# A fused attention and gated FFN kernel: loads in one ordered queue far ahead, first two batches turned in 64x64 quarters, FFN groups spread evenly

## The chip, the cores and the metric

The kernel runs on one core of one Trainium2 chip. The metric is device time in microseconds (us) from the first to the last instruction of one execution. Five engines work side by side, each through its own instructions in strict order: TensorE (PE in the profile; its weight loads are PEld), VectorE (DVE), ScalarE (ACT), GpSimd (POOL) and SyncE (SP). SyncE computes nothing here; it issues all DMA transfers. An instruction waits until the buffers it reads are filled and the buffers it writes are free, and everything behind it on its engine waits with it.

## The reference: what is computed

Eight batches of eight heads with 576 tokens and head size 64 go through causal attention with 16 extra "beacon" keys that every query may see. The result, put together over the heads (4608 tokens by 512), goes through an FFN with a ReLU gate.

```python
k_all = concat([beacon_k, k]); v_all = concat([beacon_v, v])      # per batch and head
scores = q @ k_all.T / 8, later keys masked out (never the beacons)
a = softmax(scores);  attn = a @ v_all                            # (8, 8, 576, 64)
x = attn as (4608, 512)
out = (relu(x @ w_gate) * (x @ w_val)) @ w_out                    # 512 -> 1536 -> 512, float32
```

Inputs and output are float32; matmuls run in bf16 and accumulate in float32.

## The kernel before

Everything is emitted in one hand-made order (`manual_schedule`), so the Python order is the order on each engine. Names used below:

- A **burst** is one pair of heads and one of two groups of query rows of a batch: 8 bursts a batch, 64 in all. `qk` makes the scores on TensorE, `softmax` does exp on ScalarE and masks the causal edge on GpSimd (`affine_select`), `av` multiplies with V a burst later and VectorE scales the result into `x`.
- A **tick** is one turn of the main loop: one burst, some FFN groups beside it, and loads for later batches. Bursts 0 to 7 (batch 0) come ahead of the loop, ticks 8 to 15 hold batch 1, five ticks have no burst, then batches 2 to 7 follow.
- An FFN **token tile** is 512 tokens; nine of them. Each has 12 gate/value groups (`up`, 8 matmuls of 128x128 by 512) and 4 `down` groups (12 such matmuls).

Loads come as float32 into a staging buffer `stg` and are cast to bf16. For batches 0 and 1, keys and queries are loaded a pair of heads at a time and turned by TensorE; for later batches they are loaded as row tiles ("pieces"), cast by GpSimd and turned by a DMA transpose. The attention result `x` is turned into `xT` by DMA transposes, all issued by SyncE.

```python
stage = main.enter_context(tc.tile_pool(name="stage", bufs=9))     # tiles of 128 x 768 float32
...
def pair_kq(b, p, src):                       # 96 partitions, runs of 1536 bytes
    t = stg()
    nc.sync.dma_start(t[:96].rearrange("p (h x) -> p h x", h=2),
                      src[b, 2 * p:2 * p + 2].rearrange("h (p r) d -> p h (r d)", r=R))   # R = 6
    return t

def turn_kq(t, dst, eng, cp):
    c = c16t()
    eng.tensor_copy(c[:96].rearrange("p (r h d) -> p r h d", r=R, h=2), t[:96]...)
    tp = f_ps.tile([P, R, 96], BF16, name="f")
    for r in range(R):                        # 6 transposes of 96 x 128
        nc.tensor.transpose(tp[:, r], c[:96, r * P:(r + 1) * P], ident[:96, :96])
    cp(dst.rearrange("q (p r) -> q p r", r=R), tp.rearrange("q r p -> q p r"))
# ... (cut)
def softmax(u, i):
    segs, cols = SLABS[u.g][i]                # two slabs a burst, two score buffers s_ps
    p = psb.tile([P, 2, 512], BF16, name="p")
    A.activation(p[:, :, :cols], u.s[i][:, :, :cols], AF.Exp, scale=scale)
    for (kt, q0, n, c, mask) in segs:
        if mask:
            G.affine_select(out=p[:, :, c:c + m], ...)
# ... av(u): matmuls, then VectorE; after the last pair of a group:
        if u.last:
            for qi in qt:
                r0, rn = QROWS[qi]
                nc.sync.dma_start_transpose(xT[:, :, u.b * S + r0:u.b * S + r0 + rn], u.x[:rn, qi, :])
# ... FFN
def up(nf):
    g = f_ps.tile(...)                        # 4 matmuls with wg
    A.activation(gs, g, AF.Relu)
    u = f_ps.tile(...)                        # 4 matmuls with wv
    V.tensor_mul(st["h"][:, nf, :], gs, u)
def down(ms):
    o = f_ps.tile(...)                        # 12 matmuls with wo
    A.copy(ob, o)
    nc.sync.dma_start(out[...], ob)
return [(1.74, up(nf)) for nf in range(NF)] + [(2.6, down(ms)) for ms in range(4)]   # (cost in us, emit)
```

The schedule of batches 0 and 1, and of the main loop:

```python
turn_beacons(bk, 0); pair_turn(0, 0, *loads[0])        # k cast by V, q by G
load_v_half(0, 0)                                      # V of four heads, cast by G
for s in range(8):
    u = bursts[s]; start(u); qk(u); softmax(u, 0)
    if s == 0: nxt(0, 1); load_v_half(0, 4)            # nxt: load a pair and turn it
    if s in (2, 4): nxt(0, s // 2 + 1)
    softmax(u, 1)
    if s: av(bursts[s - 1], o_ps if s % 2 else f_ps)
av(bursts[7], o_ps)                                    # then the DMA transposes of batch 0
for c, w in wq:
    if c < 2: w()(V)                                   # load gate and value weights, cast by V
# five FFN groups of tile 0, then beacons, pairs, V of batch 1 and the other weights ... (cut)
for s, u in enumerate(ticks, 8):
    if u: start(u); qk(u); softmax(u, 0)
    if prev:
        av(prev, o_ps)
        if prev.last: ...                              # a token tile becomes ready two ticks later
            ffn += [(s + 2, *g) for g in ffn_tile(m)]
    prev = u
    budget = 1.7 if s < 16 else 4.0
    spent = 0.0
    while spent < budget and ffn and ffn[0][0] <= s:   # FFN groups while there are any
        _, cost, g = ffn.pop(0); g(); spent += cost
        ...                                            # softmax(u, 1) after 1.7 us of them
    # pairs 2, 3 and V of batch 1 at s = 8, 10; three wo loads a tick from s = 10 ... (cut)
    for x in turned: piece_turn(x)                     # DMA transposes of pieces cast a tick ago
    while inflight and inflight[0][0] <= s:            # cast pieces loaded a tick or two ago (G)
        ...
    if s >= 14:                                        # load 3 pieces a tick early on, later 2
        ...
while ffn:
    if len(ffn) == 6: in_range = count_in_range()      # VectorE, TensorE, VectorE, then a register load
    ffn.pop(0)[2]()
```

The range check at the end counts rows whose sums of exp are in a sane range; a general path follows for inputs where they aren't, and isn't taken here.

Of the kernel before, what the change touches and what calls it, by code (L numbers as in the profile page):

```python
# [10 lines left out]
FP32 = mybir.dt.float32  # L11
# [131 lines left out]
def kernel(  # L143
# [15 lines left out]
    P = 128  # L159
# [9 lines left out]
    R = S // 96  # L169
# [27 lines left out]
    stage = main.enter_context(tc.tile_pool(name="stage", bufs=9))  # L197
# [9 lines left out]
    def stg():  # L207
        return stage.tile([P, 768], FP32, name="stg")

    def c16t():  # L210
        return c16.tile([P, 768], BF16, name="c16")

    V, G, A = nc.vector, nc.gpsimd, nc.scalar


    def pair_kq(b, p, src):
        t = stg()
        nc.sync.dma_start(t[:96].rearrange("p (h x) -> p h x", h=2),
                          src[b, 2 * p:2 * p + 2].rearrange("h (p r) d -> p h (r d)", r=R))
        return t  # L220

    def turn_kq(t, dst, eng, cp):
        c = c16t()
        eng.tensor_copy(c[:96].rearrange("p (r h d) -> p r h d", r=R, h=2),  # L224
                        t[:96].rearrange("p (h r d) -> p r h d", r=R, h=2))
        tp = f_ps.tile([P, R, 96], BF16, name="f")
        for r in range(R):
            nc.tensor.transpose(tp[:, r], c[:96, r * P:(r + 1) * P], ident[:96, :96])  # L228
        cp(dst.rearrange("q (p r) -> q p r", r=R), tp.rearrange("q r p -> q p r"))

    def rows_of(src, b, h0, h1, s0, s1):
        return src[b, h0:h1, s0:s1].rearrange("h p d -> p h d")

    def tile_rows(t, src, beacon, b, h0, h1, st):
        dst = st[:, :H * D].rearrange("p (h d) -> p h d", d=D)[:, h0:h1]
        if beacon is None:
            s0, n = t * P, min(P, S - t * P)
            nc.sync.dma_start(dst[:n], rows_of(src, b, h0, h1, s0, s0 + n))
            return n
        if t == 0:  # L240
            nc.sync.dma_start(dst[:Nb], rows_of(beacon, b, h0, h1, 0, Nb))
            nc.sync.dma_start(dst[Nb:], rows_of(src, b, h0, h1, 0, P - Nb))
            return P
        s0 = t * P - Nb
        n = min(P, S - s0)
        nc.sync.dma_start(dst[:n], rows_of(src, b, h0, h1, s0, s0 + n))  # L246
        return n

    def cast_v(eng, st, b, t, n, h0=0, h1=H):
        eng.tensor_copy(vs[b % 2][:n, t, h0:h1, 0:D],  # L250
                        st[:n, :H * D].rearrange("p (h d) -> p h d", d=D)[:, h0:h1])

    def load_w(dst, src, ko0, nko, n0, nn):
        t = stg()
        w = t[:, :nko * nn].rearrange("p (k n) -> p k n", k=nko)
        nc.sync.dma_start(w, src.rearrange("(ko ki) n -> ki ko n", ki=P)[:, ko0:ko0 + nko, n0:n0 + nn])
        return lambda eng: eng.tensor_copy(dst[:, ko0:ko0 + nko, n0:n0 + nn], w)  # L257
# [28 lines left out]
    def av(u, opool):  # L286
# [29 lines left out]
        if u.last:  # L316
            for qi in qt:
                r0, rn = QROWS[qi]
                nc.sync.dma_start_transpose(xT[:, :, u.b * S + r0:u.b * S + r0 + rn], u.x[:rn, qi, :])  # L319
# [38 lines left out]
    def count_in_range():  # L358

        cols = B * NP * NKT * 2  # L360
        flat = rall.rearrange("p b n t a -> p (b n t a)")
        ge = const.tile([P, cols], FP32, name="ge")
        V.tensor_scalar(out=ge, in0=flat, scalar1=1e-10, scalar2=None, op0=ALU.is_ge)
        V.scalar_tensor_tensor(out=ge, in0=flat, scalar=1e10, in1=ge, op0=ALU.is_le, op1=ALU.mult)
        ok = const.tile([P, 1], BF16, name="ok")
        V.tensor_reduce(ok, ge, op=ALU.min, axis=AX.X)
        cnt_ps = o_ps.tile([1, 1], FP32, name="o")
        nc.tensor.matmul(cnt_ps, ok, ones, start=True, stop=True)
        cnt = const.tile([1, 1], mybir.dt.int32, name="cnt")
        V.tensor_copy(cnt, cnt_ps)  # L370
        return nc.values_load(cnt, min_val=0, max_val=P,
                              skip_runtime_bounds_check_because="a count of rows")

    with tc.manual_schedule():


        def beacons_k(b):
            t = stg()
            nc.sync.dma_start(t[:Nb, :H * D].rearrange("p (h d) -> p h d", d=D), rows_of(beacon_k, b, 0, H, 0, Nb))
            return t  # L380

        def turn_beacons(t, b):
            c = c16t()
            V.tensor_copy(c[:Nb, :H * D], t[:Nb, :H * D])
            tp = f_ps.tile([P, NP, Nb], BF16, name="f")
            for p in range(NP):
                nc.tensor.transpose(tp[:, p], c[:Nb, p * P:(p + 1) * P], ident[:Nb, :Nb])
            V.tensor_copy(kTs[b % 2][:, :, 0:Nb], tp)

        def pair_turn(b, p, tk, tq):  # L390
            turn_kq(tk, kTs[b % 2][:, p, Nb:Stot], V, V.tensor_copy)
            turn_kq(tq, qTs[b % 2][:, p, :], G, V.tensor_copy)

        bursts = []
        xs = {}
# [13 lines left out]
        ffn = []  # L409

        bk = beacons_k(0)
        loads = [(pair_kq(0, 0, k), pair_kq(0, 0, q))]
        vst = {}
        def load_v_half(b, h0):
            for t in range(NKT):
                if t not in vst:
                    vst[t] = stg()
                n = tile_rows(t, v, beacon_v, b, h0, h0 + 4, vst[t])
                cast_v(G, vst[t], b, t, n, h0, h0 + 4)
            if h0:  # L420
                vst.clear()

        turn_beacons(bk, 0)
        pair_turn(0, 0, *loads[0])
        prev = None

        def nxt(b, p):
            tk, tq = pair_kq(b, p, k), pair_kq(b, p, q)
            pair_turn(b, p, tk, tq)

        wq = []
        for c in range(4):
            n0 = c * (d_ff // 4)
            for ko in (0, 2):
                for dst, src in ((wg, moe_w_gate), (wv, moe_w_val)):
                    wq.append((c, lambda dst=dst, src=src, ko=ko, n0=n0: load_w(dst, src, ko, 2, n0, d_ff // 4)))

        load_v_half(0, 0)
        for s in range(8):
            u = bursts[s]  # L440
            start(u)
            qk(u)
            softmax(u, 0)
            if s == 0:
                nxt(0, 1)
                load_v_half(0, 4)
            if s in (2, 4):
                nxt(0, s // 2 + 1)
            softmax(u, 1)
            if s:  # L450
                av(bursts[s - 1], o_ps if s % 2 else f_ps)
        av(bursts[7], o_ps)
        for c, w in wq:
            if c < 2:
                w()(V)
        ffn += [(0 if j < NF else 16, *g) for j, g in enumerate(ffn_tile(0))]
        for _ in range(5):
            ffn.pop(0)[2]()
        vst.clear()
        bk = beacons_k(1)  # L460
        turn_beacons(bk, 1)
        nxt(1, 0)
        load_v_half(1, 0)
        for c, w in wq:
            if c == 2:
                w()(V)
        nxt(1, 1)
        for c, w in wq:
            if c == 3:
                w()(V)  # L470
        wo_loads = [lambda f=f: load_w(wo, moe_w_out, f, 1, 0, d_model) for f in range(NF)]

        pieces = []
        for b in range(2, B):
            for t in range(NKT):
                for nm in "kqv":
                    pieces.append((b, t, nm))
        inflight, turned = [], []

        def piece_load(x):  # L480
            b, t, nm = x
            st = stg()
            src, be = {"k": (k, beacon_k), "q": (q, None), "v": (v, beacon_v)}[nm]
            n = tile_rows(t, src, be, b, 0, H, st)
            return (b, t, nm, n, st)

        def piece_cast(x):
            b, t, nm, n, st = x
            if nm == "v":
                cast_v(G, st, b, t, n)  # L490
                return None
            c = c16t()
            G.tensor_copy(c[:n, :d_model], st[:n, :d_model])  # L493
            return (b, t, nm, n, c)

        def piece_turn(x):
            b, t, nm, n, c = x
            dst = (kTs if nm == "k" else qTs)[b % 2]
            nc.sync.dma_start_transpose(dst[:, :, t * P:t * P + n], c[:n, :d_model])  # L499

        GAP = 5
        ticks = bursts[8:16] + [None] * GAP + bursts[16:] + [None]
        begin = {b: 8 + GAP + 8 * (b - 1) for b in range(2, B)}
        done_at = {}
        prev = None
        for s, u in enumerate(ticks, 8):
# [4 lines left out]
            if prev:  # L511
                av(prev, o_ps)
                if prev.last:
# [9 lines left out]
            while spent < budget and ffn and ffn[0][0] <= s:  # L523
# [3 lines left out]
                if sm and spent >= 1.7:  # L527
                    softmax(u, 1)
                    sm = False
# [59 lines left out]
```

## Time and profile before

| | |
|---|---|
| time, median of 2 runs | 476.27 us (475.24 to 477.31) |
| span of the profiled run | 476.1 us, 7626 instructions |
| TensorE busy | 390.8 us (82%), mean granted clock 0.896 |
| ScalarE, VectorE, GpSimd busy | 188.7, 156.9, 127.9 us |
| DMA moved | 60.17 MB, mean 126 GB/s |

The page cuts the span into 40 slices and gives the busy share of each engine in tenths; PEclk is the clock that the throttle granted to TensorE, DMA the mean share of the 16 DMA engines. A list of waits gives, for every engine, whom it waited for: total us, count, longest. An order in time has one line per group of instructions: start us, us, engine, line of the kernel, operation, out<-in, count, and in brackets the idle time before it and what ended it. SPq lines are DMA issues on SyncE. Windows give for one stretch the busy time and count of PE, PEld, DVE, ACT and POOL, then the clock, the DMA share and GB/s.

### The profile page before, as it was taken

How to read it: one execution, taken by the hardware profiler on the slowest of the kernel's cores; microseconds unless marked ns; L12 is line 12 of the kernel's file. 1: busy time of each engine (PE TensorE's matmuls, PEld its weight loads, DVE VectorE, ACT ScalarE, POOL GpSimd, SP SyncE). 2: the span in 40 equal slices, each digit the busy share in tenths (PEclk: the TensorE clock that was granted, in tenths of full speed). 3: DMA queues.
4: the chain of work that ended last, by engine and by line, in shares of the span. 5: the costliest groups of instructions: out<-in, count | busy, mean ns of one | idle time of the engine just before them, and what ended most of it. 6: DMA issues, size and time to landing. Idle time of an engine off the chain costs nothing.

```text
span 476.1 us, 7626 instructions
## 1 busy us (share of the span) xinstructions
PE 390.8 (82%) x2830; PEld 194.7 (41%) x2873; DVE 156.9 (33%) x362; ACT 188.7 (40%) x273; POOL 127.9 (27%) x288
## 2 busy tenths in 40 slices
PE   2760917889986855999999999689979998999975
PEld 1450313444432433445444544434443445544432
DVE  3441455570330121341342342224222422430430
ACT  2440202471350642454553554535453545532311
POOL 4530203233134434331432333422342212000000
PEclk9975765899997955899999999979997998999999
DMA  9507989646998789943893753966495004002002
GB/s 188 116 10 179 262 219 228 227 93 127 221 176 168 184 122 165 169 78 92 178 193 94 170 117 92 183 134 117 102 197 109 18 29 94 2 19 89 1 1 92
DMA packets 160554, 60.17 MB, mean 126 GB/s; under 512 B 147200, under 2 KB 154368, under 8 KB 160512
## 3 DMA queue, kind: packets, MB, share of 16 engines
q1 hardware_dynamic: 160512, 59.63, 60.0%
q8 instruction: 24, 0.39, 0.4%
q14 instruction: 18, 0.15, 0.1%
HBM read 38.27 MB, written 9.44 MB: 100 GB/s over the span
## 4 chain that ended last, share of the span: by engine, by line
PE 65%; DMA 14%; SPq 9%; DVE 3%; issue 3%; ACT 3%; POOL 2%; DVEq 0%; POOLq 0%; ACTq 0%
PE f L332 18%; PE f L338 18%; PE f L347 17%; PE o L304 6%; PE s L270 5%; SPq L319 4%; DMA stg<-in_v_dram 4%; DMA stg<-in_k_dram 3%; DMA xT<-x 3%; ACT p L277 2%; DMA stg<-in_q_dram 2%; SPq L246 1%; DMA stg<-in_moe_w_out_dram 1%; DMA stg<-in_moe_w_gate_dram 1%; SPq L499 1%
## 5 line engine op out<-in xcount | busy, mean ns | idle before, releaser
L332 PE MATMUL f<-xT,wg 128*128 128x512 bf16 x406 | 117.0, 404 | 23.1 <-DVE wg L257 12.5
L277 ACT ACTIVATE p<-s 128x992 bf16<-128x992 f32 (+2 forms) x128 | 107.4, 864 | 65.6 <-PE s L270 65.3
L340 DVE TENSOR_TENSOR hT<-g,f 128x512 bf16<-128x512 f32 x108 | 74.2, 688 | 147.8 <-PE f L338 133.4
L335 ACT ACTIVATE g<-f 128x512 f32<-128x512 f32 x108 | 64.5, 597 | 136.3 <-PE f L332 128.9
L338 PE MATMUL f<-xT,wv 128*128 128x512 bf16 x427 | 116.1, 394 | 1.5 <-ACT ob L350 0.8
L281 POOL TENSOR_SCALAR_AFFINE_SELECT p<-p 128x256 bf16<-128x256 bf16 (+2 forms) x160 | 61.4, 398 | 189.9 <-ACT p L277 186.2
L347 PE MATMUL f<-wo,hT 128*128 128x512 bf16 x420 | 97.1, 385 | 0.8 <-issue 0.2
L332 PEld LDWEIGHTS <-wg 128*128 128x128 bf16 x432 | 41.9, 103 | 70.4 <-DVE wg L257 13.1
L338 PEld LDWEIGHTS <-wv 128*128 128x128 bf16 x432 | 44.1, 102 | 58.3 <-issue 11.8
L304 PE MATMUL o<-vx,p 128*128 128x65 bf16 (+2 forms) x906 | 48.2, 208 | 19.0 <-POOL p L281 15.5
L347 PEld LDWEIGHTS <-hT 128*128 128x128 bf16 x432 | 42.0, 99 | 49.6 <-issue 3.0
L304 PEld LDWEIGHTS <-p 128*128 128x128 bf16 (+2 forms) x960 | 42.3, 115 | 33.5 <-POOL p L281 18.3
L312 DVE RECIPROCAL rall<-o 128x2 f32<-128x2 f32 (+2 forms) x90 | 15.7, 174 | 115.2 <-PE o L304 113.9
L350 ACT COPY ob<-f 128x512 f32<-128x512 f32 x36 | 21.1, 586 | 80.5 <-PE f L347 54.4
L270 PE MATMUL s<-qT,kT 64*128 64x208 bf16 (+4 forms) x512 | 42.0, 280 | 6.7 <-ACT p L277 5.2
L493 POOL CAST c<-stg 128x512 bf16<-128x512 f32 (+2 forms) x60 | 36.1, 613 | 40.2 <-DMA stg<-in_k_dram 28.5
L313 DVE TENSOR_TENSOR x<-o,rall 128x128 bf16<-128x128 f32 (+2 forms) x90 | 34.6, 384 | 3.3
L270 PEld LDWEIGHTS <-kT 64*128 64x128 bf16 x512 | 21.0, 102 | 30.1 <-issue 25.8
L250 POOL CAST vx<-stg 128x512 bf16<-128x512 f32 (+3 forms) x50 | 26.2, 529 | 13.9 <-DMA stg<-in_v_dram 13.7
L228 PE MATMUL f<-ident,c 96*128 96x96 bf16 x96 | 8.9, 252 | 23.0 <-DVE c L224 16.8
L224 POOL CAST c<-stg 96x768 bf16<-96x768 f32 x8 | 6.6, 822 | 40.5 <-DMA stg<-in_q_dram 40.4
L228 PEld LDWEIGHTS <-c 96*128 96x128 bf16 x96 | 6.1, 119 | 26.8 <-DVE c L224 19.5
(30 smaller groups left out, 44.8 us busy)
## 6 DMA issues: line engine op xcount, KB each, us to landing
out_dram<-ob SPq DMA_DIRECT2D x36, 256.0 KB, 2.3
stg<-in_q_dram SPq DMA_DIRECT2D x24, 256.0 KB, 4.0
stg<-in_k_dram SPq DMA_DIRECT2D x18, 256.0 KB, 3.9
stg<-in_v_dram SPq DMA_DIRECT2D x18, 256.0 KB, 4.1
stg<-in_moe_w_gate_dram SPq DMA_DIRECT2D x8, 384.0 KB, 4.6
stg<-in_moe_w_val_dram SPq DMA_DIRECT2D x8, 384.0 KB, 5.1
stg<-in_moe_w_out_dram SPq DMA_DIRECT2D x12, 256.0 KB, 5.8
stg<-in_k_dram SPq DMA_DIRECT2D x8, 288.0 KB, 4.9
```

The lines of the kernel that those rows point to most:

```text
L250: eng.tensor_copy(vs[b % 2][:n, t, h0:h1, 0:D], st[:n, :H * D].rearrange("p (h d) -> p h d", d=D)[:, h0:h1])
L270: nc.tensor.matmul(s[:, a, c:c + n], kTs[u.b % 2][rows, u.pi, kt * P:(kt + 1) * P], qTs[u.b % 2][rows, u.pi, q0:q0 + n], start=True, stop= ...
L277: A.activation(p[:, :, :cols], u.s[i][:, :, :cols], AF.Exp, scale=scale)
L281: G.affine_select(out=p[:, :, c:c + m], in_=p[:, :, c:c + m], pattern=[[0, 2], [1, m]], compare_op=ALU.is_ge, fill=0.0, base=base, channel ...
L304: nc.tensor.matmul(o[:m, j, a, 0:D + 1], p[:kr, a, c:c + m], vs[u.b % 2][:kr, kt, 2 * u.pi + a, 0:D + 1], start=first, stop=(kt == kts[-1] ...
L313: V.tensor_mul(u.x[:m, i0:i0 + j1 - j0, u.pi * P:(u.pi + 1) * P].rearrange("p j (a d) -> p j a d", a=2), o[:m, j0:j1, :, 0:D], r.unsqueeze ...
L332: nc.tensor.matmul(g, wg[:, ki, nf * P:(nf + 1) * P], xT[:, ki, m0:m0 + M_TILE], start=(ki == 0), stop=(ki == KM - 1))
L335: A.activation(gs, g, AF.Relu)
L338: nc.tensor.matmul(u, wv[:, ki, nf * P:(nf + 1) * P], xT[:, ki, m0:m0 + M_TILE], start=(ki == 0), stop=(ki == KM - 1))
L340: V.tensor_mul(st["h"][:, nf, :], gs, u)
L347: nc.tensor.matmul(o, st["h"][:, nf, ms * P:(ms + 1) * P], wo[:, nf, :], start=(nf == 0), stop=(nf == NF - 1))
L493: G.tensor_copy(c[:n, :d_model], st[:n, :d_model])
```

## The change

Five things are changed together.

1. **Loads in one ordered list.** Every load of batches 0 and 1 and of all weights becomes a `Load` object with `issue`, `cast` and `turn`. They stand in one list `todo`; `pump` issues from it while fewer than 14 are open (the pool has 14 smaller buffers of 128 x 576 instead of 9 of 128 x 768). A load is thus emitted as soon as a buffer's earlier user is cast, far ahead of its use. No transposing DMA stands between these loads.
2. **Longer runs and quarter transposes.** A pair of heads is loaded on 128 partitions in runs of 2304 bytes (9 rows of one head), weights in runs of 2048 bytes. A pair's tile is then turned by 18 transposes of 64x64 instead of 6 of 96x128, each head in its own half of the partitions.
3. **Batch 0's `x` is turned by TensorE**, copied by VectorE and ScalarE, instead of five DMA transposes.
4. **FFN groups spread evenly.** Each tick's share of FFN work is the work left up to the next tile that becomes ready, divided by the ticks to it (at most 4.6 us), rather than 4.0 us while there is any.
5. **The range check** is split and started earlier, so its register load comes three groups after its matmul.

Casts move as well: half of the weights (`wv`, and half of `wo`) are cast by GpSimd; the first q is cast by ScalarE, which also does the copies of later q's in batch 1; V is cast for all heads at once; `softmax(u, 1)` comes ahead of the pair turns in batch 0, and after the first FFN group in the loop.

```diff
-    R = S // 96
+    R = 2 * S // P
-    stage = main.enter_context(tc.tile_pool(name="stage", bufs=9))
+    NSTG = 14
+    stage = main.enter_context(tc.tile_pool(name="stage", bufs=NSTG))
 ...
+            if self.kind == "pair":
+                src, b, p = self.key
+                dma(st, src[b, 2 * p:2 * p + 2].rearrange("h (p r) d -> (h p) (r d)", r=R))
+            elif self.kind == "w":
+                dst, src, ko, n0 = self.key
+                dma(st[:, :512], src[ko * P:(ko + 1) * P, n0:n0 + 512])
 ...
+                tp = f_ps.tile([P, R, D], BF16, name="f")
+                for r in range(R):
+                    for a in range(2):
+                        rows = slice(a * D, (a + 1) * D)
+                        nc.tensor.transpose(tp[rows, r], c[rows, r * D:(r + 1) * D], ident[rows, rows])
 ...
-                nc.sync.dma_start_transpose(xT[:, :, u.b * S + r0:u.b * S + r0 + rn], u.x[:rn, qi, :])
+                dst = xT[:, :, u.b * S + r0:u.b * S + r0 + rn]
+                if u.b:
+                    nc.sync.dma_start_transpose(dst, u.x[:rn, qi, :])
+                    continue
+                tp = f_ps.tile([P, KM, P], BF16, name="f")
+                for ki in range(KM):
+                    nc.tensor.transpose(tp[:, ki, :rn], u.x[:rn, qi, ki * P:(ki + 1) * P], ident[:rn, :rn])
+                (V.tensor_copy if qi % 2 else A.copy)(dst, tp[:, :, :rn])
 ...
+        todo = (pq[0, 0] + [bk[0]] + pq[0, 1] + vl[0] + pq[0, 2] + pq[0, 3] + ch[0]
+                + [bk[1]] + pq[1, 0] + ch[1] + pq[1, 1] + vl[1] + ch[2] + pq[1, 2] + pq[1, 3] + wol)
+        def pump():
+            while todo and Load.open < NSTG:
+                todo.pop(0).issue()
+        def pair_turn(b, p, ke, qe, kc, qc):
+            tk, tq = pq[b, p]
+            tk.cast(ke).turn(kc)
+            tq.cast(qe).turn(qc)
+            pump()
 ...                                          # batch 0
+            softmax(u, 0)
+            softmax(u, 1)
+            if s == 0:
+                pair_turn(0, 1, V, G, V.tensor_copy, V.tensor_copy)
+                for x in vl[0]: x.cast(G)
+                pump()
+            elif s in (2, 4):
+                pair_turn(0, s // 2 + 1, V, G, V.tensor_copy, V.tensor_copy)
+            if s: av(bursts[s - 1], o_ps if s % 2 else f_ps)
+            if s >= 5:                        # first chunk of gate and value weights
+                for x in ch[0][(s - 5) * 3:(s - 4) * 3]: x.cast(V if x.key[0] is wg else G)
 ...                                          # main loop
+        def budget(s):
+            if s < T0 + 8:
+                return 1.7
+            best = 4.6
+            for r in sorted(set(ready.values())):
+                if r > s:
+                    best = min(best, sum(c for t, c, _ in ffn if t < r) / (r - s))
+            return best
-            while spent < budget and ffn and ffn[0][0] <= s:
+            want += budget(s)
+            while ffn and ffn[0][0] <= s and spent + ffn[0][1] / 2 <= want:
 ...
-            if s >= 14:
+            if not todo:                      # pieces start when the list is empty
                 early = s < begin[2]
                 for _ in range(3 if early else 2):
-                    if pieces and (early or s >= begin[pieces[0][0]] - 10):
+                    if pieces and Load.open < NSTG and (early or s >= begin[pieces[0].key[2]] - 10):
 ...
-            if len(ffn) == 6:
-                in_range = count_in_range()
+            if len(ffn) == 10: range_flags()
+            if len(ffn) == 8:  range_count()
+            if len(ffn) == 5:  in_range = nc.values_load(cnt, ...)
```

The diff is cut to its core; the cuts are marked with `...`, and a few lines are joined. In batch 1, pairs 1, 2, 3 are turned in ticks 8, 10, 12; the second weight chunk is cast ahead of tick 8, the third in tick 10, and `wo` by fours from tick 13.

## The prediction

> **What bounds the kernel now.** I read the page's slices first, then TensorE's waits, then the orders in time of SyncE, GpSimd and TensorE, and last the windows with the DMA rate.
>
> ```profile
> PE   2760917889986855999999999689979998999975
> PEclk9975765899997955899999999979997998999999
> DMA  9507989646998789943893753966495004002002
> ```
>
> Each digit covers 11.9 us. TensorE is full from about slice 17 on; its holes lie in slices 0 to 16 (0 to 200 us), with small ones near 306 and 355 us. The granted clock sinks in and after each hole, so a hole is paid for twice. The waits of TensorE (total us, count, longest) name the causes:
>
> ```profile
> PE f L228 <- DVE c L224: 16.8, 8, 7.6
> PE o L304 <- POOL p L281: 15.5, 9, 5.0
> PE f L332 <- DVE wg L257: 12.5, 2, 11.1
> PE f L332 <- DMA xT<-x: 7.9, 3, 4.2
> ```
>
> These are a K/Q load not there yet, a mask not applied yet, gate weights not there yet, and a transposed token tile not there yet. SyncE's own order shows why the weights are late:
>
> ```profile
> 12.39 0.40 SPq L218 DMA_DIRECT2D stg<-in_q_dram  x1
> 33.41 7.32 SPq L319 DMA_TRANSPOSE xT<-x  x5
> 40.83 0.53 SPq L256 DMA_DIRECT2D stg<-in_moe_w_gate_dram  x1
> ```
>
> From 12.8 to 33.4 us SyncE issues nothing: it stands at the five transposes of batch 0, behind which the weight loads are queued. GpSimd's order shows the second trouble, the refill of batches 2 and 3:
>
> ```profile
> 124.90 0.62 POOL L493 CAST c<-stg 128x512 bf16<-128x512 f32 x1 [6.24 <-DMA stg<-in_k_dram]
> 131.68 0.62 POOL L493 CAST c<-stg 128x512 bf16<-128x512 f32 x1 [3.94 <-DMA stg<-in_k_dram]
> 141.95 0.61 POOL L493 CAST c<-stg 128x512 bf16<-128x512 f32 x1 [2.99 <-DMA stg<-in_k_dram]
> 146.13 1.10 POOL L281 TENSOR_SCALAR_AFFINE_SELECT p<-p 128x224 bf16<-128x224 bf16 x3
> ```
>
> Rounds of three casts come 5 to 7 us apart, and the mask of the first burst of batch 2 stands behind six of them. TensorE's order shows what this costs, and how cold matmuls look beside warm ones:
>
> ```profile
> 48.50 1.91 PE L338 MATMUL f<-xT,wv 128*128 128x512 bf16 x4
> 99.82 1.03 PE L332 MATMUL f<-xT,wg 128*128 128x512 bf16 x4
> 146.57 0.35 PE L304 MATMUL o<-vx,p 128*128 128x65 bf16 x3 [4.99 <-POOL p L281]
> 188.00 0.58 PE L332 MATMUL f<-xT,wg 128*128 128x512 bf16 x1 [1.09 <-DMA xT<-x]
> 311.38 0.59 PE L332 MATMUL f<-xT,wg 128*128 128x512 bf16 x1 [4.16 <-DMA xT<-x]
> ```
>
> The marks I use are: first FFN matmul 45.6, end of batch 1's attention 108.6, first matmul of token tile 2 at 188.0, last matmul 471.2, end 476.1.
>
> **What the Trainium skill says.** (1) "TensorE: Matmul & The Clock Gate", the part on the HAM clock gate: an idle window of about 3.4 us drops the clock to half. The trace agrees: four matmuls took 1.91 us after the 11.1 us wait, 1.03 us later. (2) "DMA: Bandwidth & Descriptors", Specifications: runs under 512 B lose rate. It agrees. In the windows (times of five engines, clock, DMA share, GB/s) the first is a mix with V's 256-byte runs, the second weights in 1536-byte runs:
>
> ```profile
> 10.00:12.00 2.00, 0.66 (x6) 0.45 (x6) 1.25 (x2) 0.45 (x1) 1.91 (x4) 1.00 1.38 214
> 50.00:52.00 2.00, 2.00 (x6) 0.69 (x5) 1.07 (x2) 0.00 (x0) 0.00 (x0) 0.50 1.11 374
> ```
>
> (3) The same page, "Anatomy of one DMA": a DMA's semaphore wait is held on the issuing sequencer. The 20.6 us of silence on SyncE is that. (4) "TensorEngine Tiling (Array Packing)", Key Properties: different tiles can work in parallel. No quarter transposes are in this trace, so I give them little credit.
>
> **The change, stage by stage.**
>
> *Stage 1, to the first FFN matmul.* All loads for two batches and all weights form one list over 14 slots with no transpose in between, and batch 0 is turned by TensorE. The first weight chunk then waits only for slots and should be on chip before batch 0 ends; the 11.1 us wait goes. Against that, batch 0 itself gets slower. Each pair's transposes go from 12 to 36. Twelve of 96x96 took 2 x 0.66 us; the four 16x16 took 0.27 us, of which about 0.17 is latency, so 18 quarters should take about 1.0 us: +0.7 us a pair. GpSimd's cast of q now stands behind both masks of its burst (one more 0.4 us select and the shorter exp), and V's whole cast (5 x 0.61) stands before the mask of burst 1. I add 1 us for the first pair and about 1.6 us each for two later ones: batch 0's last AV moves from 34.5 to about 38.5. Twenty transposes, five copies (about 0.7 us, as for 128x576 here) and the last x multiply make 2.5 us. First FFN matmul: about 41, instead of 45.6.
>
> *Stage 2, to the end of batch 1.* Four FFN groups at 1.73 us plus 3 for the cold start end near 50. Before the first burst stand the beacon (cast 0.41, turn 0.3, copy 0.2), cast of k (0.45), 1 us of transposes and a 0.76 us copy behind the last hT multiply: about 5 us, so burst 8 starts at 55. A plain tick with one FFN group took 3.0 to 3.5 us before (98.67, 101.64, 105.13). A pair turn adds about 3.5, and the tick that also casts four gate chunks (4 x 0.46) about 5.5. Ticks 8 to 15: 7 + 4 + 9 + 3.5 + 7 + 3.3 + 3.3 + 4.5 = 41.6. Batch 1 ends near 96, against 108.6. The DMA is not in the way: 14.2 MB of pairs and weights in long runs at about 340 GB/s (the windows from 44 to 52 us show 330 to 374) is 42 us, 2.4 MB of V at about 210 is 11, in all less than the stages have.
>
> *Stage 3, to token tile 2.* Here little is gained. Between the last x of batch 1's first group and tile 2, before, SyncE issued 30 transposes at about 1.31 us with the gap and 35 loads at about 0.62, plus 8 stores: 65 us of issue in 78 us. The order of the changed program still has 28 transposes and 30 loads there (36.7 + 18.3), plus 6 stores (3.3) = 58 us. Worse, refill pieces start two ticks earlier, so 26 casts instead of 18 stand on GpSimd before the mask of burst 16, while only 4 downs and 4 gate/value groups (10.4 + 6.9 us) stand on TensorE between the end of batch 1 and that burst's AV. To the load of the 26th piece there are 17 transposes, 20 loads and 4 stores: 22.3 + 12.2 + 2.8 = 37 us, plus 4 of landing and 2 of casting, from about 92.5: mask at 135 to 137. TensorE arrives at about 113. So I expect one hole of some 20 us where there were several small ones. After it come nine ticks with FFN spread at 2.78 plus 1.07 for the burst, 3.85 each: 35 us. Tile 2 starts near 172 or 173, against 188: the gain of stage 2 and a little more.
>
> *Stage 4, to the end.* Before, 476.1 - 188.0 = 288.1. Warm work is 7 tiles x 144 matmuls x 0.216 = 217.7; 37.5 bursts at 1.07 (three groups and a burst took 6.08 and 6.41 us, less 3 x 1.727) = 40; tail 4.9: together 262.6. The other 25 are holes at 303-311 (5.6), 352-358 (4.0), 402 (1.2), the range check (2.9), and the cold and unmixed stretches after them. They come from using up the FFN groups and then waiting for the transposes of x. The even spread keeps groups for every tick, so tile starts are met with some 15 us of slack; the range check is moved ahead of use. I keep 2.4 for one cold start: 265.
>
> Sum: 173 + 265 = **438 us**, 38 less than now: about 15 from the early loads, 23 from the spread.
>
> **Rivals.** *A, the refill keeps up.* If GpSimd's casts are not held by SyncE, tile 2 starts at 96 + 10.4 + 3.5 + 10 x 3.85 = 148 and the end is near 413. Against it: DMA is 0.8 to 1.1 busy in slices 10 to 12, and SyncE works nearly without pause there. *B, batch 0 and 1 get no faster.* Quarter transposes cost more than 1 us a tensor, casts queue on GpSimd (now also half of the weights, 0.61 each against 0.46 on VectorE), and stage 2 ends at 108 again: end near 450. For it: GpSimd's order is strict, and every burst's mask passes through it. *C, the spread moves holes instead of filling them.* If ticks 21 to 30 with 2.78 us of FFN become bound by SyncE and later ticks of 5 us by the refill (15 transposes at 1.31 and 17 loads at 0.62 make about 30 us of issue per 8 ticks of 39), stage 4 keeps 10 us of holes and C with B ends near 460. Against it: with ticks of 6 us from 200 to 300 us TensorE hardly waited.
>
> **Range and chances.** My 438 lies between A (413) and B (450). Each stage may be off by about 8 us, mostly independently, which makes 14 or so; I put the range that holds 8 times in 10 at 416 to 456. To be within 2% the time would have to be above 466.7, which needs B and C together and more: 6%. Slower needs a new wait I do not see: 3%. Faster by over 2%: 91%.
>
> **What would show it.** Right: the gate weights no longer in TensorE's waits; first FFN matmul at 38 to 44; end of batch 1 at 90 to 100; one AV wait on the mask of about 20 us at 113 to 137; tile 2 at 165 to 180; no wait on x transposes after 200 us. Wrong: the mask wait of burst 16 under 8 us (then A), pair turns of over 5 us (B), waits on x transposes at tile starts (C).

## The result and the profile after

The changed kernel takes 442.3 us, the median of two runs (440.3 to 444.3), against 476.3 before: a ratio of 0.929, 95% interval 0.908 to 0.949. The prediction said 438 (416 to 456). The total was right; its parts were off by up to 6.5 us, and their errors cancelled. The profiled run has a span of 438.5 us at a mean granted clock of 0.964 (before 476.1 and 0.896).

The slices of the page first, 11.0 us to a digit:

```profile
PE   3668658784649979999999899999989989999995
PEclk9989988996859999999999999999999999999999
DMA  9954894798995278973984697559872012002002
```

TensorE is full (8 or more) from slice 12 (132 us) on but for a 7 in slice 14 and the tail; before it was from slice 16 (190 us), with a 6 and a 7 later. The dips that remain after the first two batches are in slices 9 to 11, 99 to 132 us: the stretch between the end of batch 1 and the first bursts of batch 2. The clock falls there too.

TensorE's waits in the changed kernel (total us, count, longest):

```profile
PE f L272 <- DVE c L260: 16.4, 7, 4.7
PE o L330 <- POOL p L307: 13.7, 7, 9.8
PE s L296 <- ACT p L303: 9.6, 12, 1.2
PE f L365 <- ACT ob L383: 4.8, 1, 4.8
```

Two waits of before are gone: the gate weights (12.5 us) and the transposed x (7.9). Waiting for a cast K or Q tile costs what it did (16.8 then). The mask wait also has its old total (15.5 then), but 9.8 us of it are now one hole. And the wait on `ob`, the buffer of a finished output tile, has grown from 0.8 to 4.8 us. TensorE's order in time shows where they lie:

```profile
36.04 1.02 PE L365 MATMUL f<-xT,wg 128*128 128x512 bf16 x4 [0.51 <-ACT xT L352]
...
99.44 1.81 PE L365 MATMUL f<-xT,wg 128*128 128x512 bf16 x4 [2.24 <-issue]
...
108.03 1.87 PE L365 MATMUL f<-xT,wg 128*128 128x512 bf16 x4 [4.82 <-ACT ob L383]
...
126.52 0.35 PE L330 MATMUL o<-vx,p 128*128 128x65 bf16 x3 [9.76 <-POOL p L307]
...
169.63 1.02 PE L365 MATMUL f<-xT,wg 128*128 128x512 bf16 x4
```

Read it as marks: the first FFN matmul at 36.0 (before 45.6), the first AV of batch 2 (burst 16) at 126.5 after an idle time of 9.8 us, token tile 2 at 169.6 (before 188.0). The four matmuls at 108 take 1.87 us, those at 36 and 169 only 1.02: after the hole they run cold. SyncE's order explains both waits. (First number start, second the time of the issue.)

```profile
12.39 0.36 SPq L233 DMA_DIRECT2D stg<-in_moe_w_gate_dram  x1
...
94.34 0.82 SPq L245 DMA_DIRECT2D stg<-in_q_dram  x1
95.26 2.98 SPq L347 DMA_TRANSPOSE xT<-x  x2
98.33 0.53 SPq L384 DMA_DIRECT2D out_dram<-ob  x1
98.97 1.22 SPq L283 DMA_TRANSPOSE kT<-c  x1
```

The first gate weights are issued at 12.4 us, where before they were issued at 40.8. But from 86 us on the queue has no gap: the store of the first output tile, whose data were ready at about 90 us, goes out at 98.3, behind loads and transposes. ScalarE pays for it, as its order shows; the bracket is its own wait:

```profile
100.84 0.58 ACT L383 COPY ob<-f 128x512 f32<-128x512 f32 x1 [8.18 <-DMA out_dram<-ob]
...
107.40 0.58 ACT L383 COPY ob<-f 128x512 f32<-128x512 f32 x1 [5.97 <-DMA out_dram<-ob]
```

Only two `ob` buffers exist; the third output copy waits for the first store and the fourth for the second, and TensorE's 4.8 us are the wait for that fourth copy. What ended its 2.2 us at 99.4 the trace does not say (`issue`); it is the first matmul of token tile 1, and at the same matmul of e2 (below) the trace names a transpose of x, for 2.9 us. GpSimd's order shows what the 9.8 us wait for:

```profile
125.52 0.61 POOL L260 CAST c<-stg 128x512 bf16<-128x512 f32 x1 [0.46 <-DMA stg<-in_q_dram]
126.08 1.10 POOL L307 TENSOR_SCALAR_AFFINE_SELECT p<-p 128x224 bf16<-128x224 bf16 x3
```

The mask of burst 16 comes directly behind the 23rd of the refill's casts, and that cast was waiting for its load.

### The profile page after: what moved, and what is told of

It reads as the page before. It is cut to its first block, busy times and chain, and to the rows that moved or that the text cites. A ratio compares the mean times of both kernels' runs of the same rounds, so it can differ in the third digit from the quotient of the medians.

```text
span 438.5 us, 8104 instructions
## 1 busy us (share of the span) xinstructions
PE 377.0 (86%) x3085; PEld 187.2 (43%) x3085; DVE 150.3 (34%) x349; ACT 193.2 (44%) x282; POOL 134.6 (31%) x295
## 5 line engine op out<-in xcount | busy, mean ns | idle before, releaser
L303 ACT ACTIVATE p<-s 128x992 bf16<-128x992 f32 (+2 forms) x128 | 108.3, 864 | 35.5 <-PE s L296 33.5
L365 PE MATMUL f<-xT,wg 128*128 128x512 bf16 x432 | 114.8, 389 | 7.6 <-ACT ob L383 4.8
L371 PE MATMUL f<-xT,wv 128*128 128x512 bf16 x432 | 113.8, 387 | 0.2 <-ACT ob L383 0.2
L365 PEld LDWEIGHTS <-wg 128*128 128x128 bf16 x432 | 40.2, 100 | 51.4 <-issue 11.6
L330 PE MATMUL o<-vx,p 128*128 128x65 bf16 (+2 forms) x888 | 43.8, 200 | 14.2 <-POOL p L307 13.7
L330 PEld LDWEIGHTS <-p 128*128 128x128 bf16 (+2 forms) x960 | 38.9, 109 | 27.4 <-POOL p L307 15.3
L296 PE MATMUL s<-qT,kT 64*128 64x208 bf16 (+4 forms) x512 | 39.0, 265 | 11.0 <-ACT p L303 9.6
L260 POOL CAST c<-stg 128x512 bf16<-128x512 f32 (+2 forms) x67 | 40.9, 622 | 8.5 <-DMA stg<-in_k_dram 4.9
L256 POOL CAST vx<-stg 128x512 bf16<-128x512 f32 (+1 forms) x40 | 24.4, 616 | 25.0 <-DMA stg<-in_v_dram 25.0
L272 PE MATMUL f<-ident,c 64*64 64x64 bf16 x288 | 8.7, 220 | 20.6 <-DVE c L260 16.4
L272 PEld LDWEIGHTS <-c 64*64 64x64 bf16 x288 | 7.2, 132 | 23.5 <-DVE c L260 18.8
L274 ACT COPY qT<-f 128x576 bf16<-128x576 bf16 x5 | 3.2, 638 | 14.0 <-PE f L272 14.0
```

Of the source, the lines that this page charges most:

```text
L256: cp(vs[b % 2][:n, t, :, 0:D], self.st[:n, :H * D].rearrange("p (h d) -> p h d", d=D))
L260: cp(c[:n, :w], self.st[:n, :w])
L296: nc.tensor.matmul(s[:, a, c:c + n], kTs[u.b % 2][rows, u.pi, kt * P:(kt + 1) * P], qTs[u.b % 2][rows, u.pi, q0:q0 + n], start=True, stop= ...
L330: nc.tensor.matmul(o[:m, j, a, 0:D + 1], p[:kr, a, c:c + m], vs[u.b % 2][:kr, kt, 2 * u.pi + a, 0:D + 1], start=first, stop=(kt == kts[-1] ...
L365: nc.tensor.matmul(g, wg[:, ki, nf * P:(nf + 1) * P], xT[:, ki, m0:m0 + M_TILE], start=(ki == 0), stop=(ki == KM - 1))
L371: nc.tensor.matmul(u, wv[:, ki, nf * P:(nf + 1) * P], xT[:, ki, m0:m0 + M_TILE], start=(ki == 0), stop=(ki == KM - 1))
```

## The experiments

The changed kernel was run again beside the first variants: 446.5 us (445.2 to 449.8), ratio 0.941 with an interval of 0.931 to 0.951. What was expected of it:

> The changed kernel once more, to have an interval beside the ones below. All theories: 440 to 444 us, first FFN matmul near 36, tile 2 near 170.

It came out slower than expected, with the first FFN matmul at 39.0 and tile 2 at 175.1. All comparisons are with this run and, since not all ran on one chip, by the ratio to the kernel before on the same chip. Single times more than 1.5% above the fastest of the same kernel (two of e8's four, one of e5's, and the profiled one of e4 with e5, which the table therefore lacks) are left out of the ratios, which leaves e8 too few for an interval. The table gives marks of the profiled runs, each read from TensorE's order in time. "End of batch 1" is the first `down` matmul; 3a is from there to the AV of burst 16, 3b from there to tile 2, 4 from tile 2 to the end of the span. Up to the end of batch 1 several of the variants are the same program as the changed kernel and still differ by up to 5 us from profile to profile (86.7 to 91.6), so differences of that size in the first two columns mean nothing. The two profiles of the changed kernel agree within 0.7 us in 3a and 0.1 us in 3b and 4. In the second one the AV of burst 16 stands so, and its 10.9 us are what the variants below are compared with:

```profile
132.06 0.35 PE L330 MATMUL o<-vx,p 128*128 128x65 bf16 x3 [10.85 <-POOL p L307]
```

| kernel | first FFN | end of batch 1 | 3a | 3b | 4 | span | ratio |
|---|---|---|---|---|---|---|---|
| before | 45.6 | 108.5 | 38.1 | 41.4 | 288.1 | 476.1 | 1 |
| changed | 36.0 | 86.7 | 39.8 | 43.1 | 268.9 | 438.5 | 0.929 |
| changed, again | 39.0 | 91.6 | 40.5 | 43.0 | 268.9 | 444.0 | 0.941 |
| e1: no spread | 36.2 | 88.4 | 39.8 | 33.2 | 283.3 | 444.7 | 0.937 |
| e2: batch 0's x by DMA | 43.0 | 95.2 | 40.3 | 47.6 | 268.4 | 451.5 | 0.958 |
| e3: 96-row loads and turns | 36.2 | 93.3 | 37.3 | 42.9 | 268.8 | 442.3 | 0.935 |
| e7: 9 buffers | 38.4 | 94.4 | 37.1 | 42.8 | 268.6 | 442.9 | 0.938 |
| e4: batch 3 held back | 37.3 | 90.5 | 32.4 | 42.5 | 268.5 | 434.0 | 0.917 |
| e5: stores by ScalarE | 37.2 | 89.0 | 38.4 | 46.8 | 271.0 | 445.2 | 0.937 |
| e8: gap filled | 37.0 | 89.9 | 40.2 | 35.7 | 267.5 | 433.3 | about 0.91 (no interval) |
| e9: e8 and e4 | 36.6 | 90.0 | 33.1 | 36.2 | 267.6 | 427.0 | 0.903 |
| e10: e9, batch 1's x by TensorE | 35.8 | 89.7 | 30.5 | 34.6 | 267.0 | 421.8 | 0.899 |
| b1: before with spread only | 46.2 | 108.5 | 36.8 | 42.6 | 274.9 | 462.8 | 0.971 |

**e1, the spread undone.** All else is the changed kernel.

```diff
-            want += budget(s)
+            spent, want = 0.0, 1.7 if s < T0 + 8 else 4.0
-            while ffn and ffn[0][0] <= s and spent + ffn[0][1] / 2 <= want:
+            while ffn and ffn[0][0] <= s and spent < want:
```

> Only the even spread is undone: 4.0 us of FFN a tick while there is any, as before. Theory (spread is worth what the stage from tile 2 to the end gained, 19 us): 458 to 464 us, with waits of TensorE on transposes of x back at tile starts, 3 to 5 us each. Rival (the spread only moves the holes; the gain of that stage came from loads further ahead): 440 to 448 us.

Measured: 445.7 us (445.0 to 446.4), ratio 0.937 (0.928 to 0.946): the same as with the spread. TensorE's waits in e1:

```profile
PE o L330 <- POOL p L307: 10.6, 7, 3.9
...
PE f L365 <- DMA xT<-x: 7.2, 3, 3.9
```

The waits on transposed x are back, as the spread was meant to remove them: stage 4 is 14.4 us longer. But 3b is 9.8 us shorter. Without the spread all twelve groups of tile 1 run before the AV of burst 16 (nine in the gap without bursts, three beside that burst's scores), and its hole shrinks from 10.9 to 3.9 us; with the spread four run before it (two and two) and eight are kept for later. Mark 3a is the same 40 us in both. So the time is the rival's, but the waits and the loss in stage 4 are the theory's. The spread is no gain of 23 us here: it saves 14 late and gives 10 back early. The 4 to 5 us that remain by the marks do not show in the whole.

**b1, the spread alone,** in the kernel before (the same two rules of readiness and budget, nothing else).

> The kernel before with the even spread alone, nothing else of the change. The prediction's term (23 us from the spread): 450 to 456 us, ratio 0.945 to 0.96. Theory S (about 14 to 19 saved after the start of tile 2, 3 to 8 given back in the gap before it): 460 to 468, ratio 0.965 to 0.985, token tile 2 later than 188 us, no wait of the FFN on x after 200 us. If the spread is worth nothing without the early loads: 473 to 478, ratio 0.99 to 1.005.

Measured: 461.8 us (458.4 to 464.6), ratio 0.971 (0.963 to 0.978). Here it brings 13.6 us, 13.2 of them in stage 4, and 3a and 3b together stay at 79.4: nothing is given back, unlike expected. The kernel before had little left to do in 3b, but its bare bursts after the gap waited for the refill there, in the kernel before three times for a mask, 2.1 us and these two:

```profile
179.02 1.12 PE L304 MATMUL o<-vx,p 128*128 128x65 bf16 x15 [3.08 <-POOL p L281]
...
185.51 0.35 PE L304 MATMUL o<-vx,p 128*128 128x65 bf16 x3 [2.74 <-POOL p L281]
```

In b1 the groups kept back fill these waits. Stage 4 of b1 is still 6 us above the changed kernel's. TensorE's order in b1 shows the reason:

```profile
439.76 0.16 PE L368 MATMUL o<-ones,ok 128*1 128x1 bf16 x1 [2.14 <-DVE ok L366]
440.66 1.86 PE L332 MATMUL f<-xT,wg 128*128 128x512 bf16 x4 [0.74 <-DVE cnt L370]
```

That is the range check: two waits of 2.9 us together, and cold matmuls behind them. In the changed kernel the same matmul has no wait:

```profile
415.86 0.16 PE L404 MATMUL o<-ones,ok 128*1 128x1 bf16 x1
```

The last tile's gate/value groups took 27.0 us in b1 and 21.0 in the changed kernel. So of the 19.2 us of stage 4 some 13 to 14 are the spread, in both kernels. The other 5 to 6 are put down to the moved check by these traces; it was not moved alone in any run.

**e2, batch 0's x by DMA transposes again.**

```diff
-                if u.b:
+                if True:
                     nc.sync.dma_start_transpose(dst, u.x[:rn, qi, :])
```

> Only the turning of batch 0's x is undone: five DMA transposes on SyncE instead of TensorE. Theory (the order of the list, weights ahead of the transposes, is what the first stage gained by): first FFN matmul at 40 to 42 instead of 36, gate weights still not among TensorE's waits, 3 to 7 us more in all. Rival (it is TensorE's turning that took away the wait): first FFN matmul at 45 or later, 10 us more in all.

Measured: 454.9 us (453.5 to 456.6), ratio 0.958 (0.949 to 0.967), 8.4 us more than the changed kernel beside it. TensorE's order in e2:

```profile
33.97 1.12 PE L330 MATMUL f<-vx,p 128*128 128x65 bf16 x15 [0.45 <-POOL p L307]
43.01 0.59 PE L365 MATMUL f<-xT,wg 128*128 128x512 bf16 x1 [7.91 <-DMA xT<-x]
```

The last AV of batch 0 ends at 35.1 (34.3 and 37.2 in the changed kernel's two profiles), but the FFN starts after 7.9 us of waiting for transposes. The gate weights are still not among TensorE's waits, as the theory has it; the first FFN matmul at 43.0 and the loss of 8.4 us lie between theory and rival. The first FFN matmul is 4.0 us later than in the run beside it and still 2.6 earlier than in the kernel before, with some 3 us of scatter between profiles. 3b is longer too, by 4.6 us, with a second mask wait of 2.9 us in it; why was not pursued. So this part of the change pays, but only about half of what it pays is explained.

**e3, loads and turns as before** (96 partitions, runs of 1536 bytes, six 96x128 transposes, 12 larger buffers), **and e7, nine buffers.** In both, a cast whose load isn't issued yet issues it first.

```diff
-    R = 2 * S // P
+    R = S // 96
...  (e3: pair loads, casts and transposes of the kernel before, stage tiles of 768)
-    NSTG = 14
+    NSTG = 12        # e3;   9 in e7
```

> Only the form of the pair loads and transposes is undone: 96 partitions in runs of 1536 bytes, 6 transposes of 96x128; 12 slots[...]. Theory (quarters cost nothing and gain little: 18 of them took 0.69 us, six of the other form 0.66): 0 to 4 us more, from casts of 768 columns instead of 576. Rival of the prediction (quarters cost 0.7 us a pair more): 2 to 6 us less.

> Nine slots in the list instead of 14, same order. Theory (being far ahead matters): weights and V of batch 1 come later, end of batch 1 at 93 to 100 instead of 87, 5 to 12 us more in all. Rival (order alone matters, depth is spare): end of batch 1 within 2 us, total within 3 us.

Measured: e3 443.8 us, ratio 0.935 (0.930 to 0.940); e7 445.4, 0.938 (0.928 to 0.947). Neither differs from the changed kernel (0.941, 0.931 to 0.951). Longer runs with quarters, and the depth of 14, are worth nothing that shows in the whole. For the depth that is what the rival said; the two forecasts for e3 lie too close together to be told apart here.

**e4, batch 3's pieces held back** until ten ticks ahead of their batch, so that 18 casts stand ahead of burst 16's mask. (In the changed kernel 23 do, by its program and its trace, and not 26 as the prediction and the text below count.)

```diff
-  if pieces and Load.open < NSTG and (early or s >= begin[pieces[0].key[2]] - 10):
+  if pieces and Load.open < NSTG and ((early and pieces[0].key[2] == 2) or s >= begin[pieces[0].key[2]] - 10):
```

> Pieces of batch 3 are held back to tick 19, so 18 casts instead of 26 stand on GpSimd ahead of the mask of burst 16. Theory G (the order on GpSimd makes the 9.8 us hole): the hole shrinks to under 3 us and 6 to 11 us are saved. Theory S (SyncE's issue time up to tile 2 is the bound): the hole moves to bursts 17 to 25 and the time stays within 3 us. Theory O (stores queued behind transposes on SyncE, which hold ScalarE and with it TensorE at 97 to 108 us): those 7 us of waits stay in both cases.

Measured: 435.3 us (434.1 to 436.5), ratio 0.917 (0.912 to 0.922). TensorE's order in e4:

```profile
111.55 1.86 PE L365 MATMUL f<-xT,wg 128*128 128x512 bf16 x4 [5.32 <-ACT ob L383]
...
122.92 0.35 PE L330 MATMUL o<-vx,p 128*128 128x65 bf16 x3 [3.39 <-POOL p L307]
```

The mask hole falls from 10.9 to 3.4 us (a little less than theory G said) and 3a from 40.5 to 32.4; 3b and 4 are unchanged, so the hole does not move to later bursts as in theory S. The store wait stays. The refill ahead of the mask is what sets 3a. The edit takes both casts on GpSimd and issues on SyncE from ahead of that mask; moving the mask alone ahead of the casts was not tried.

**e5, stores issued by ScalarE, and e4 with e5 together.**

```diff
-                nc.sync.dma_start(out[m0 + ms * P:m0 + (ms + 1) * P, :], ob)
+                nc.scalar.dma_start(out[m0 + ms * P:m0 + (ms + 1) * P, :], ob)
```

> Output stores are issued by ScalarE right after its copy instead of by SyncE. Theory O: ScalarE's waits of 8.2 and 6.0 us on the stores and TensorE's of 2.2 and 4.8 us on ScalarE go. Theory G or S: TensorE then only arrives earlier at the mask of burst 16, whose time is set by SyncE; the hole there grows from 9.8 to 16 to 20 us and the time falls by 5 us at most (fewer issues on SyncE). If stores were the whole bound: 10 to 14 us less.

> Both of the last two. Theory G plus O: both holes go, 14 to 22 us less than the changed kernel (420 to 428 us), more than the two apart together. Theory S: 3 to 6 us less, with new waits on K and Q of batch 3 or on x.

Measured: e5 446.3 us (443.8 to 452.2), ratio 0.937 (0.930 to 0.944), no gain; both together 438.3, ratio 0.922 (0.917 to 0.927), no better than e4 alone and, at some 9 us less than the changed kernel, between the two forecasts. TensorE's waits in e5:

```profile
PE o L330 <- POOL p L307: 19.8, 6, 16.7
...
PE s L296 <- ACT p L303: 13.2, 12, 1.6
```

The store wait is gone, and the mask hole has grown from 10.9 to 16.7 us, as theories G and S said: TensorE comes earlier to a mask that comes only 2 us sooner. The time lost to the store was not on the path; it was the first part of the same hole. And the scores now wait longer for exp (13.2 us, in the changed kernel 9.6), presumably since the issue stands on ScalarE: 3b grows by 4.

**e8, the gap filled and the spread kept** from the first tick of batch 2 on.

```diff
-            if s == T0 + 8:
+            if s in (T0 + 8, T0 + 8 + GAP):
                 spent = want = 0.0
-            want += budget(s)
+            want += 5.2 if T0 + 8 <= s < T0 + 8 + GAP else budget(s)
```

> Only the gap changes: in the five ticks without a burst the FFN budget is 5.2 us a tick, so nine groups of token tile 1 go there, where the changed kernel has four; from the first tick of batch 2 on the even spread is as it was. Theory S (the spread saves in stage 4 what it says, but gave part back by withholding groups in the gap): the AV wait of burst 16 falls from about 10 us to 4 to 6, token tile 2 starts at 161 to 167, stage 4 stays at 267 to 272, in all 430 to 438 us, ratio 0.905 to 0.92. Rival R (SyncE's refill sets when tile 2 can start, wherever the groups stand): the nine groups are missing from the ticks after the gap, new waits appear there, tile 2 starts at 172 to 175 as before, in all 442 to 447, ratio 0.93 to 0.94.

Measured: 435.8 us (430.1 to 440.1) over all four times, 430.1 and 435.0 in the two that count. Tile 2 starts at 165.8, 3b is 35.7 and stage 4 267.5: theory S. One number of it missed: the AV wait of burst 16 is 7.6 us, not 4 to 6; filling the gap does nothing to 3a (40.2). (The text above gives the changed kernel four groups in the gap; two of these stand beside the scores of burst 16.)

**e9, e8 with e4, and e10, batch 1's x turned by TensorE too** (`if u.b > 1` for the DMA transposes).

> The gap filled as in e8 and batch 3's pieces held to tick 19 as in e4. If the two are one gain taken in two ways (both fill the same hole at burst 16): within 2 us of the better of e8 and e4, ratio 0.91 to 0.917, tile 2 at 162 to 166. If they add: tile 2 at 156 to 160, 426 to 431 us, ratio 0.897 to 0.907. The AV wait of burst 16 under 2 us in either case.

> e9, and batch 1's x turned by TensorE too: five transposes of about 1.3 us leave SyncE's queue just ahead of the refill, 20 transposes and five copies (some 2.5 us) come to TensorE and the copying engines. If SyncE's queue still sets the start of batch 2: 2 to 5 us less than e9, and the wait for an output tile's store shorter than 4 us. If not: the same as e9 within 2 us, or 1 to 2 us more.

Measured: e9 428.4 us (427.5 to 429.3), ratio 0.903 (0.897 to 0.908). The two gains add stage by stage: 3a is short as in e4, 3b as in e8, and tile 2 starts at 159.4. In the whole the ratio falls by 0.038 from the changed kernel's, less than the 0.024 of e4 and 0.03 of e8 together. e10 425.6 us (422.9 to 429.0), ratio 0.899 (0.890 to 0.908); its times overlap with e9's, but 3a and 3b are 4.2 us shorter together, and ScalarE's wait of 6.7 us for a store is gone. The mask waits in e9 and e10, from TensorE's waits, first e9:

```profile
PE o L330 <- POOL p L307: 4.6, 7, 1.8
```

and e10:

```profile
PE o L330 <- POOL p L307: 1.7, 4, 0.6
```

Of 13.7 us, 1.7 are left. e10 is faster than both kernels, with the changed kernel's arithmetic.

## Why the prediction was right, and where its steps were not

Its stages added up to 41 + 55 + 76.5 + 265; measured are 36.0, 50.6, 83.0 and 268.9. The differences, -5.0, -4.4, +6.5 and +3.9, sum to 1. That they cancel is luck, and more so since the first two move from profile to profile: in the second profile of the changed kernel they are -2.0, -2.4, +7.0 and +3.9, 6.5 in all.

**Stage 1.** The mechanism held: gate weights no longer wait, the start is set by batch 0 itself. The term that was too large is the slowdown of batch 0, from 34.5 to 38.5: its last AV ended at 34.3, in the second profile at 37.2. Eighteen quarter transposes took 0.69 us against 0.66 for six of 96x96, not 1.0. TensorE waited 3.8 us for GpSimd's casts of q, no more than before (4.4). The longest wait of batch 0 is one that the prediction did not name: 3.2 us (4.9 in the second profile) for the k of the third pair, whose load is issued behind those of V. And turning x took 1.7 us instead of 2.5, since its first three row tiles went beside the last burst.

**Stage 2.** The predicted ticks, 41.6 us, took 40.0 (46.7 to 86.7). The rest of the error is mostly the cold start of 3 us, which did not come: the first FFN groups ran at 1.03 us for four matmuls. In the second profile half of it came: the first eight took 3.3 us, eight warm ones 1.7. The Trainium skill has the clock fall to half after an idle window of about 3.4 us ("TensorE: Matmul & The Clock Gate", the part on the HAM clock gate), and e2 agrees: after 7.9 us of idling, four took 1.91 us. The second profile shows that slow matmuls here don't need such a window right before them: none of TensorE's waits in the 12 us ahead of its slow start is longer than 0.6 us.

**Stage 3.** The refill as what holds the mask was right. The prediction laid 17 transposes, 20 loads and 4 stores, 37 us of issue, before the mask. From 86.3 us, where the transposes of x begin, to burst 16's AV the trace has just these, 17 transposes (22.5 us), 20 loads (12.3) and 4 stores (3.3): 38.1 of 40.2 us. But the mask stands behind 23 casts and not 26, and the last five of the 41 come after the load for the 23rd; the other 36 took 35.5 us. In exchange the transposes of x began 0.3 us before the end of batch 1 and not 3.5. So 3a, 39.8 us for 40 predicted, is right by two errors of some 3 us. e4 and e10 confirm the cause: with 14 transposes and 15 loads 3a fell to 32.4, with 8 and 15 to 30.5 (there SyncE is busy for 25.9 only, and TensorE has no wait left above 0.15 us, so its own work sets the length). Wrong was the size of the one hole, about 20 us: it was 9.8, because TensorE arrived later, 30 us after the end of batch 1 instead of 17. It lost 5.0 us to the store buffers (0.2 and 4.8), 2.2 to what looks like a transpose of x, and some 4 to slow matmuls behind these waits. The store wait was not named. It cost nothing on its own, as e5 shows.

The term that failed in stage 3 is the last: nine ticks at 3.85 us after the mask. They took 43.1 us, 35 predicted. The prediction took the work of groups and a burst; a tick with one `down` group (2.76 us) has in addition a wait for exp of 0.9 to 1.1, as in four of these nine, for example:

```profile
153.91 0.35 PE L296 MATMUL s<-qT,kT 64*128 64x208 bf16 x4 [1.12 <-ACT p L303]
```

These are 4.0 us; further waits for masks are 1.6, and the first tick runs cold, 1.3 us. The rest, some 1.5 us, was not taken apart. e8 and e1 shorten just this part, by 7 and 10 us, by having fewer groups left in it.

**Stage 4.** 268.9 instead of 265, and the sum's "23 from the spread" is not right as a cause. In e1 and b1 the spread is worth 13 to 14 us in this stage, and the moved range check, by the traces, most of the other 5 to 6. As a whole the spread brings 13.6 us to the kernel before and nothing that shows to the changed one, where it takes FFN work out of the gap while TensorE waits there. That interaction was not in the prediction.

**The rivals.** A (413, the refill keeps up) was wrong for the changed kernel, yet e9 and e10 move towards it by shortening the refill and filling the gap. B (450, batches 0 and 1 no faster) is wrong: their end came 22 us earlier (17 in the second run). C is wrong for stage 4, where no wait on x is left, but something like it happened in stage 3.

**What stays open.** e2 gives 8.4 us to turning x on TensorE, b1 13.6 to the spread (in the old kernel), e3 and e7 nothing to runs, quarters and depth. The rest of the 30 to 34 us belongs to the one ordered list without transposes between loads, to the moved casts and to the range check; the list alone was not tried. The traces show where the early gain lies, not which part of the change brings it: up to the first FFN matmul TensorE stood idle for 15.1 us instead of 26.0, and from there to the end of batch 1 for 13.7 instead of 19.4, at a granted clock of 0.93 instead of 0.75.

## What to carry to other kernels

An even spread of filler work pays where each later stretch has its own holes; before a stretch in which the critical engine waits for a refill in any case, spend the filler there and start the even spread after it. A refill that begins earlier is not sooner done if its casts stand on the in-order engine ahead of the work that is due: load what the next batch needs and hold the batch after it back. And before removing a wait, look at what ends next: the store wait here was the front of a longer one.

## What the runs showed of the hardware

Eighteen 64x64 transposes of bf16, alternating between two quarters of the array, took 0.69 us cold and 0.47 warm, nearly as little as six of 96x96 (0.66 and 0.43): 26 ns each when warm. The Trainium skill says that different tiles of the array can work in parallel ("TensorEngine Tiling (Array Packing)", Key Properties); the times fit that but do not show it, since no run here tried the same quarters on one half alone. A DMA transpose held SyncE for 1.2 us of issue and more (22.5 us for 17), a plain load for some 0.6 (12.3 for 20), so in the stretch where SyncE set the pace the transposes took most of it.
